# Attention, then a gated feed-forward block: another order of the kernel's 1094 steps, and one bias product in place of a mask product

## The chip, the cores and the metric

The kernel runs on one core of one Trainium2 chip. The metric is the time of one execution in microseconds of device time: the kernel before takes 238.46 us (median of 3 runs, 238.38 to 238.53).

## What is computed

The first half is attention over 4 batches, 8 heads, 768 positions and 64 channels. A query sees the 96 positions up to and with its own and the first 8 positions of the sequence ("global" keys); each score carries a bias, minus a slope of the head times the distance. The second half takes the attention output as 3072 tokens of 512 channels through two 512 x 1536 products, multiplies `silu` of the one with the other, and through a 1536 x 512 product.

```python
scores = scale * np.matmul(q, k.transpose(0, 1, 3, 2))
keep = is_global | is_local
bias = -slopes[:, None, None] * dist[None, :, :]
scores = np.where(keep, scores + bias[None], -1000000000.0)
a = np.exp(scores - max); a = a / (sum(a) + 1e-09)
x = np.matmul(a, v)                     # -> (3072, 512)
g = x @ w_gate
out = (g / (1 + np.exp(-g))) * (x @ w_val) @ w_out
```

## The kernel before, in words

**Tiling.** Keys are cut into chunks of 120, each with the 8 global keys beside it. For a batch and a pair of heads the scores of all chunks lie in three or four units: four in batch 0, where a unit holds up to 432 columns for each of two heads, three in the later batches. Scores lie with the keys on the partitions, so the exponentials go straight into the product with `v`. The feed-forward half works on 8 blocks of 384 tokens (two to a batch) and 12 blocks of 128 hidden channels.

**Order.** Nothing schedules this program but the constant `ORDER` (L39 to L123): a list of 1094 steps, run from the first to the last (L715 to L717). Each step issues its instructions on one engine (a few on two), each engine and each DMA queue runs its own in the order in which they were issued, and waits only for data and for buffers. Another list is another order on every engine. The list also decides which of the 8 banks of PSUM a product gets: `single` and `double` (L225 to L241) hand out banks that a step earlier in the list gave back, so a product waits for the instruction that last read its bank.

**The steps**, with their line and engine. Numbers after the letter are batch or token block, pair of heads, unit, and so on.

- Loads: `Ld`, `Li`, `Lf.S` on the SyncE queue and `Lf.A` on the ScalarE queue (distance table, identity, and the first half of `q` and `k` of the heads 0 to 3 in float32; L252 to L259); `Lh`, `Lv`, `Lw`, `L4`, `Lr`, `Lo` on GpSimd's queue (the rest of `q` and `k` of batch 0, `v`, the weights, later batches; L262 to L319).
- `pre` (L323 to L326, VectorE): sets a tile of ones and zeroes parts of the key tiles. `zc` (L517, L518): zeroes the corners of the buffers for the exponentials, `zc.1` of five buffers in ten instructions. `Z` (L282): zeroes parts of a `v` tile.
- `fill.n` (L343, TensorE): n products of the tile of ones, which nobody reads; they keep TensorE at work while it has no data.
- `cast` (L347): float32 to float16 of what `Lf` loaded. `sl.h` (L329, VectorE): the identity times the slope of head h. `M.h.part` (L335, ScalarE): the mask of head h, the exponential of minus slope times distance; part 0 has 216 columns, part 1 has 432.
- `T` (L364, TensorE): six transposes of `q` or `k`; `k`, `q` (L377 to L383, L393): copy them out of PSUM, on the engine named at the end (V is VectorE, A is ScalarE, P is GpSimd). `G`: copies the global rows of `v` into the other chunks.
- `B.hp.u` (L461, TensorE): the bias of a unit of batch 0, slope-identity times distance table, summed into the scores' bank ahead of them. `c` (L481): the scores. `x` (L526, ScalarE): the exponential. `m` (L553, VectorE): the product with the mask, for the units that had no `B`. So every unit of batch 0 has either four small matmuls of `B` or one to two VectorE instructions of `m`.
- `w` (L585, TensorE): sums and weighted `v`; `i`, `r` (L604, L605, L611): the reciprocal of the sums, spread over the rows; `n` (L597): copies the weighted sums out; `p` (L621): multiplies them into the token block `xT`.
- `g`, `v` (L638, TensorE): gate and value product of a token block and a block of hidden channels, four matmuls each (`ga`, `gb`: the halves of a `g`); `t` (L644, ScalarE): tanh; `s` (L648, VectorE): silu, which frees the bank of `g` and the buffer of `t` (there are three); `h` (L654, VectorE): times the value product, which frees the bank of `v` and the buffer of `s`.
- `o` (L679, L668, TensorE): the product with `w_out`; `e` (L697, L688, L692): copies it out and stores it. `D`, `K`, `U`, `kw`, `qw`: keys and queries of the later batches, by DMA transposes or by TensorE.

In what follows the *head* is all that comes before step `g.0.3`, and the *stream* is the rest, where TensorE goes through the same kinds of product to the end.

Of the kernel before, what the change touches and what calls it, by code (L numbers as in the profile page):

```python
# [55 lines left out]
s.0.5 Lr.1.0.6 v.0.7 Lv.1.3 g.0.11 s.0.6 h.0.3 Lr.1.1.4 h.0.5 t.0.4 s.0.4 h.0.7 Lr.1.0.5 m.0.3.2.V
v.0.4 h.0.4 g.0.9 Lr.1.1.7 g.0.10 t.0.9 w.0.0.1.1 w.0.0.1.2 t.0.10 Lr.1.0.4 h.0.6 s.0.9 t.0.11
w.0.1.1.0 w.0.1.1.1 s.0.10 w.0.1.1.2 p.0.0.1.0.V Lo.2 i.0.1.1 v.0.2 p.0.0.1.1.V r.0.1.1 p.0.1.1.0.V
v.0.9 p.0.1.1.1.V Lr.2.0.0 v.0.10 g.0.8 v.0.11 g.1.4 g.1.6 t.0.8 D.1.2.0 s.0.8 h.0.9 Lr.2.0.1 g.1.1
h.0.10 t.1.4 t.1.1 h.0.2 g.1.8 s.1.4 g.1.5 s.0.11 U.0.0 U.0.1 D.1.2.1 s.1.1 U.1.1 t.1.8 U.1.0  # L60
Lr.1.0.7 h.0.11 v.1.4 s.1.8 t.1.6 kw.0.A v.1.6 qw.1.A kw.1.V g.1.0 s.1.6 v.1.8 h.1.4 qw.0.A h.1.6
t.1.0 Lv.1.2 s.1.0 c.1.0.1 c.1.1.0 v.0.8 g.1.9 t.1.5 h.1.8 x.1.1.0 s.1.5 t.1.9 x.1.0.1 v.1.1 g.1.2
h.0.8 o.0.1.0 D.1.3.0 s.1.9 c.1.1.1 Lr.3.0.1 c.1.0.0 x.1.1.1 Lr.2.1.3 v.1.0 h.1.1 o.0.0.0 o.0.1.1
x.1.0.0 g.1.7 t.1.2 t.1.7 v.1.9 Lr.2.0.2 Lr.2.0.3 h.1.0 m.1.0.0.V g.1.3 g.1.11 Lr.2.1.2 v.1.3 s.1.2
o.0.0.1 m.1.1.1.V v.1.11 o.0.0.2 t.1.11 o.0.1.2 s.1.7 m.1.0.1.V D.1.3.1 Lr.2.1.0 v.1.2 s.1.11 t.1.3
h.1.11 o.0.0.3 s.1.3 h.1.9 o.0.1.3 m.1.1.0.V w.1.0.0.2 w.1.0.0.1 h.1.3 e.0.0 h.1.2 K.1.2 w.1.0.0.0
c.1.2.1 e.0.1 c.1.2.0 o.0.2.0 n.1.0.0 x.1.2.1 i.1.0.0 g.1.10 Lr.2.0.5 K.1.3 r.1.0.0 x.1.2.0 v.1.5
Lr.2.1.5 o.0.2.1 o.0.2.2 h.1.5 t.1.10 Lv.1.4 c.1.3.1 p.1.0.0.0.V x.1.3.1 Lv.1.5 D.2.0.0 s.1.10
m.1.2.0.V m.1.2.1.V m.1.3.1.V c.1.3.0 v.1.7 Lv.1.6 v.1.10 o.1.0.0 o.0.2.3 x.1.3.0 e.0.2 Lr.2.1.4
D.2.1.0 m.1.3.0.V o.1.0.1 c.1.0.2 w.1.1.0.0 w.1.1.0.1 w.1.1.0.2 h.1.7 Z.2.P p.1.0.0.1.V o.1.1.0  # L70
o.1.0.2 x.1.0.2 h.1.10 Lr.3.0.0 i.1.1.0 c.1.2.2 c.1.1.2 Lr.2.0.4 n.1.1.0 K.2.0 x.1.2.2 c.1.3.2
o.1.1.1 x.1.3.2 r.1.1.0 o.1.1.2 Lr.2.1.1 Lr.2.1.6 D.2.1.1 p.1.1.0.1.V Lr.2.0.7 p.1.1.0.0.V o.1.0.3
m.1.2.2.V g.2.6 Lr.2.0.6 t.2.6 g.2.10 g.2.2 v.2.2 o.1.1.3 t.2.10 e.1.0 t.2.2 s.2.6 v.2.6 s.2.10
m.1.0.2.V g.2.0 g.2.5 m.1.3.2.V s.2.2 x.1.1.2 g.2.9 h.2.2 t.2.0 Lr.3.0.4 v.2.0 m.1.1.2.V h.2.6
w.1.0.1.1 w.1.0.1.0 w.1.0.1.2 t.2.5 Lr.3.1.4 Lv.2.4 s.2.5 s.2.0 w.1.1.1.1 e.1.1 w.1.1.1.0 Lv.2.0
n.1.0.1 i.1.0.1 w.1.1.1.2 Lr.3.1.1 Lr.3.0.5 o.1.2.0 g.2.7 r.1.0.1 t.2.9 D.2.0.1 i.1.1.1 D.2.2.0
v.2.7 n.1.1.1 t.2.7 r.1.1.1 Lr.2.1.7 o.1.2.1 Lr.3.1.0 s.2.7 g.2.3 t.2.3 p.1.1.1.0.V v.2.5 Lr.3.0.7
D.2.3.0 Lv.2.1 v.2.4 v.2.9 o.1.2.2 h.2.7 h.2.5 p.1.0.1.0.V Lr.3.0.2 s.2.9 h.2.9 Lr.3.0.3 o.1.2.3
# [28 lines left out]
h.5.0 o.4.2.0 m.3.0.2.V s.5.5 t.5.3 t.5.2 s.5.3 o.4.0.3 g.6.0 v.5.11 s.5.2 h.5.11 v.5.3 m.3.2.2.V
t.5.9 v.5.1 s.5.6 o.4.2.1 h.5.1 g.5.4 h.5.3 o.4.2.2 s.5.9 v.5.2 v.5.9 m.3.3.2.V h.5.2 o.4.2.3 h.5.9
g.6.8 g.6.11 t.5.4 v.5.5 e.4.0 g.6.10 t.6.0 s.6.0 t.6.8 s.5.4 h.5.5 w.3.1.1.0 w.3.0.1.1 w.3.0.1.0
w.3.0.1.2 s.6.8 e.4.2 w.3.1.1.1 i.3.1.1 w.3.1.1.2 v.6.8 i.3.0.1 t.6.10 n.3.0.1 v.5.4 g.6.2 n.3.1.1  # L110
# [642 lines left out]
```

## Time and profile before

| | |
|---|---|
| time, median of 3 runs | 238.46 us (238.38 to 238.53) |
| the profiled execution | 238.79 us |
| its span, first to last instruction | 237.0 us |
| TensorE (PE) busy | 229.5 us, 97% |
| VectorE (DVE) busy | 173.8 us, 73% |
| ScalarE (ACT) busy | 138.0 us, 58% |
| GpSimd (POOL) busy | 77.6 us, 33% |
| moved by DMA | 25.54 MB |

The span is 1.8 us shorter than the execution's own time. The profile shows each matmul from its start to a modelled end, so that matmuls overlap: a busy PE says that none of them was waited for longer than the tail of the one before, and only the distance from one start to the next tells how fast they go. PEld, the loading of weights, overlaps PE. In rows of the timeline, the first two numbers are the start and the length in us, "x6" are six instructions in one row, and a bracket at the end gives idle time ahead of the row and what ended it.

### The profile page before, as it was taken

The page shows a single profiled execution, that of the slowest core. Times are in us where ns is not written, and L with a number is a line of the kernel's source. Part 1 is how long each engine was busy: PE and PEld are TensorE (multiplying, and loading weights), DVE is VectorE, ACT ScalarE, POOL GpSimd, SP SyncE. Part 2 cuts the span into 40 slices and gives each one's busy share as a digit, 9 for nine tenths or more (in the row PEclk, how much of TensorE's full clock was granted, in tenths as well). Part 3 has the DMA queues.
Part 4 walks back from the last instruction along what each step waited for, and adds up shares of the span by engine and source line. Part 5 has one row for each costly group of instructions (what it writes and reads, how often), then busy time and mean ns, then how long its engine had stood idle before and what let it go on. Part 6 is the DMA issues. An engine that isn't in the chain of part 4 may idle for free.

```text
span 237.0 us, 6183 instructions
## 1 busy us (share of the span) xinstructions
PE 229.5 (97%) x2520; PEld 132.3 (56%) x2520; DVE 173.8 (73%) x428; ACT 138.0 (58%) x251; POOL 77.6 (33%) x102
## 2 busy tenths in 40 slices
PE   3999999999999999999999999999999999999994
PEld 2655666655555655555655564565556655555442
DVE  6799898948786888877988988776679984364400
ACT  6699632792889624778983389969334222412131
POOL 8975585540969774665300000000000000000000
PEclk9999999999999999999999999999999999999999
DMA  7999999999999999999995150011011000110034
GB/s 177 181 182 207 193 198 186 176 176 162 139 130 153 178 165 139 141 167 112 139 192 55 44 80 27 20 47 47 0 44 48 3 1 0 44 47 0 8 125 177
DMA packets 88196, 25.54 MB, mean 108 GB/s; under 512 B 78016, under 2 KB 85224, under 8 KB 88168
## 3 DMA queue, kind: packets, MB, share of 16 engines
q0 software_dynamic: 66992, 13.77, 74.6%
q1 hardware_dynamic: 20488, 10.80, 24.9%
q10 hardware_dynamic: 688, 0.59, 0.7%
q8 instruction: 19, 0.31, 0.5%
q14 instruction: 9, 0.07, 0.1%
HBM read 28.51 MB, written 6.29 MB: 147 GB/s over the span
## 4 chain that ended last, share of the span: by engine, by line
PE 94%; DVE 3%; ACT 1%; issue 1%; DVEq 0%
PE banks L638 53%; PE banks L679 26%; PE banks L585 6%; PE banks L481 4%; PE banks L343 2%; PE banks L668 1%; PE banks L364 1%; ACT at L526 1%; PE banks L461 1%; PE banks L402 1%; DVE at L518 0%; DVE rb L611 0%; DVE at L517 0%; DVE dT L604 0%; DVE xT L621 0%
## 5 line engine op out<-in xcount | busy, mean ns | idle before, releaser
L644 ACT ACTIVATE th<-banks 128x384 f32<-128x384 f32 x96 | 44.1, 491 | 60.1 <-PE banks L638 54.6
L638 PE MATMUL banks<-xT,wv 128*128 128x384 f16 x384 | 73.3, 326 | 0.0
L638 PE MATMUL banks<-xT,wg 128*128 128x384 f16 x384 | 72.1, 326 | 0.0
L654 DVE TENSOR_TENSOR hT<-banks,sl 128x384 f16<-128x384 f32 x96 | 51.3, 551 | 24.0 <-PE banks L638 22.2
L679 PE MATMUL banks<-wo,hT 128*128 128x512 f16 x276 | 68.5, 379 | 0.0
L526 ACT ACTIVATE at<-banks 64x640 f16<-64x640 f32 (+4 forms) x88 | 62.3, 714 | 5.3 <-PE banks L481 4.3
L648 DVE SCALAR_TENSOR_TENSOR sl<-th,banks 128x384 f32<-128x384 f32 x96 | 50.8, 547 | 12.6 <-ACT th L644 11.6
L638 PEld LDWEIGHTS <-wg 128*128 128x128 f16 x384 | 37.3, 98 | 27.0
L638 PEld LDWEIGHTS <-wv 128*128 128x128 f16 x384 | 36.4, 98 | 26.6
L679 PEld LDWEIGHTS <-hT 128*128 128x128 f16 x276 | 26.1, 98 | 26.5
L553 DVE TENSOR_TENSOR at<-at,masks 128x864 f16<-128x864 f16 (+5 forms) x62 | 26.1, 459 | 4.5 <-ACT at L526 4.4
L267 POOL DMA_DIRECT2D vS<-in_v_dram x28 | 25.0, 899 | 10.3 <-DMA vS<-in_v_dram 3.0
L697 ACT ACTIVATE osb<-banks 128x512 f32<-128x512 f32 x23 | 13.6, 597 | 22.1 <-PE banks L679 18.4
L305 POOL DMA_DIRECT2D kst<-in_k_dram x20 | 16.7, 841 | 14.1 <-DMA kN<-kst 8.8
L305 POOL DMA_DIRECT2D qst<-in_q_dram x20 | 16.8, 846 | 7.5 <-DMA qst<-in_q_dram 2.6
L481 PE MATMUL banks<-qT,kT 64*64 64x160 f16 (+9 forms) x408 | 13.3, 227 | 0.2 <-DVE xT L621 0.2
L481 PEld LDWEIGHTS <-kT 64*64 64x64 f16 (+1 forms) x408 | 7.9, 104 | 8.9 <-issue 7.6
L621 DVE TENSOR_TENSOR xT<-ns,rb 128x384 f16<-128x384 f32 x24 | 12.5, 550 | 0.3
L585 PE MATMUL banks<-at,vS 128*32 128x216 f16 (+6 forms) x576 | 12.0, 225 | 0.1
L597 ACT COPY ns<-banks 128x768 f32<-128x768 f32 x12 | 9.4, 801 | 4.5 <-PE banks L585 4.2
L604 DVE STREAM_TRANSPOSE dT<-banks 128x384 f32<-128x384 f32 x16 | 9.2, 574 | 3.1 <-PE banks L585 2.8
L585 PEld LDWEIGHTS <-vS 128*32 128x32 f16 x576 | 10.0, 95 | 2.3 <-issue 1.5
(59 smaller groups left out, 116.7 us busy)
## 6 DMA issues: line engine op xcount, KB each, us to landing
out_dram<-osb SPq DMA_DIRECT2D x23, 256.0 KB, 2.1
vS<-in_v_dram POOLq DMA_DIRECT2D x24, 120.0 KB, 8.0
qst<-in_q_dram POOLq DMA_DIRECT2D x20, 96.0 KB, 8.5
kst<-in_k_dram POOLq DMA_DIRECT2D x20, 96.0 KB, 7.9
wg<-in_moe_w_gate_dram POOLq DMA_DIRECT2D x6, 256.0 KB, 9.3
wv<-in_moe_w_val_dram POOLq DMA_DIRECT2D x6, 256.0 KB, 8.3
wo<-in_moe_w_out_dram POOLq DMA_DIRECT2D x3, 512.0 KB, 10.3
k<-in_k_dram POOLq DMA_DIRECT2D x3, 192.0 KB, 6.3
```

The lines of the kernel that those rows point to most:

```text
L267: nc.gpsimd.dma_start(out=v_of(b)[r0:r0 + n, c, :, :], in_=v[b, :, KC * c:KC * c + n, :].rearrange("h p d -> p h d"))
L305: nc.gpsimd.dma_start(out=rows_of(i, b, h // 2)[:, :, h % 2, :], in_=KQ[i][b, h].rearrange("(t p) d -> p t d", p=128))
L481: nc.tensor.matmul(sc[k0:k1, hi, col + a:col + z], lhsT=keys[r, k0:k1], rhs=qTs[b, hp][r, q0 + a:q0 + z], start=fresh, stop=True, skip_gro ...
L526: nc.scalar.activation(out=of(at), in_=of(sc), func=AF.Exp, scale=scale)
L553: ENG[e].tensor_mul(a2, a2, m[:, :, m0:m0 + n])
L585: nc.tensor.matmul(dst[r, o:o + n], lhsT=vSs[b][:, c, 4 * g + j, what - 1::2] if what else ones[:, 0:32], rhs=ats[b, hp, u][:, j % 2, col: ...
L638: nc.tensor.matmul(gv[t, f, which][:, 0:TB], lhsT=w[:, c, 128 * f:128 * f + 128], rhs=xTs[t][:, c, :], start=(c == 0), stop=(c == NC - 1))
L644: nc.scalar.activation(out=th, in_=gv[t, f, 0][:, 0:TB], func=AF.Tanh, scale=0.5)
L648: nc.vector.scalar_tensor_tensor(out=sl, in0=gv[t, f, "t"], scalar=1.0, in1=gv[t, f, 0][:, 0:TB], op0=AluOp.add, op1=AluOp.mult)
L654: nc.vector.tensor_mul(hTs[t][:, f, :], gv[t, f, 1][:, 0:TB], gv[t, f, "s"])
L679: nc.tensor.matmul(ops_t[t, i], lhsT=hTs[t][:, f, 128 * i:128 * i + 128], rhs=wo[:, f, :], start=(f == 0), stop=(f == NFF - 1))
L697: nc.scalar.mul(out=osb, in_=ops, mul=0.5)
```

## The change

Only `ORDER` is changed. The list has 1094 steps before and after. In batch 0, `B.0.1` and `B.2.1` come in, and `B.3.1` goes; `m.0.0.1.V` and `m.0.2.1.V` go, and `m.0.3.1.V` comes in: one bias product more, one mask product less. All other steps are the same, in another sequence from the first line to the last. The part that is spoken of most is the beginning (before, then after):

```diff
-Ld.S Z.0.P Z.3.P Lf.A.1.1 Li zc.0.V Lh.0.0.4.8 zc.1.V Lf.A.1.0 Lh.1.0.4.8 pre cast.1.1.V Lf.S.0.1
-M.5.1 M.0.0 sl.3 Lf.S.0.0 M.2.1 Lh.1.1.0.4 fill.14 sl.7 M.1.0 sl.6 Lh.0.1.0.4 Z.1.V sl.2 cast.0.1.V
-M.7.0 T.1.0.1 B.1.1 q.1.0.V M.3.1 cast.1.0.P T.1.0.0 Lh.1.1.4.8 cast.0.0.A M.2.0 fill.2 Lv.0.1
-k.1.0.V sl.1 M.7.1 T.0.0.0 T.2.0.0 k.0.0.V Lv.0.0 T.3.0.0 sl.0 k.3.0.V M.4.1 M.5.0 B.1.0 M.0.1
-T.0.0.1 c.0.1.1 Lh.0.1.4.8 sl.4 T.2.0.1 M.3.0 c.0.1.0 q.0.0.V x.0.1.1 Lv.0.2 q.2.0.V T.1.1.1 T.3.0.1
-M.6.0 B.0.0 k.2.0.V x.0.1.0 Lv.0.3 c.0.0.0 sl.5 M.1.1 Lw.0.0.1 c.0.0.1 T.1.1.0 x.0.0.1 q.3.0.V M.4.0
...
-w.0.0.1.0 s.0.2 t.0.0 s.0.0 c.0.3.3 Lw.1.2.0 x.0.2.3 i.0.0.1 c.0.3.2 v.0.0 g.0.3 t.0.1 x.0.3.3
...
+Lf.A.1.1 Ld.S Lf.A.1.0 Z.0.P M.6.1 pre Li M.0.1 Z.3.P Lh.1.0.4.8 Lf.S.0.1 zc.1.V Lf.S.0.0 Z.1.V
+zc.0.V Lh.0.0.4.8 fill.14 cast.1.1.V Lh.0.1.0.4 sl.3 T.1.0.1 sl.2 M.3.1 M.2.1 sl.5 Lh.1.1.0.4
+cast.1.0.P cast.0.1.V q.1.0.V sl.6 B.1.0 B.1.1 M.7.1 sl.1 sl.0 cast.0.0.A Lv.0.0 M.1.1 T.1.0.0
+T.0.0.1 M.5.1 fill.2 T.0.0.0 T.3.0.1 k.1.0.V sl.7 k.0.0.V Lv.0.3 c.0.1.1 T.2.0.1 M.5.0 c.0.1.0 M.2.0
+x.0.1.1 q.3.0.V M.7.0 x.0.1.0 q.2.0.V B.0.1 q.0.0.V Lh.1.1.4.8 M.0.0 T.3.0.0 T.2.0.0 T.0.1.0 sl.4
+c.0.0.1 k.2.0.V Lh.0.1.4.8 T.1.1.0 B.0.0 Lv.0.2 c.0.0.0 x.0.0.1 B.2.0 M.3.0 c.0.2.0 M.1.0 T.0.1.1
+k.3.0.V x.0.0.0 Lv.0.1 Lw.0.0.0 k.1.1.V Lw.0.0.1 B.2.1 x.0.2.0 c.0.2.1 T.1.1.1 x.0.2.1 M.4.0 k.0.1.V
+zc.2.V w.0.0.0.0 c.0.3.1 M.6.0 B.3.0 q.0.1.A c.0.3.0 T.2.1.1 x.0.3.1 G.0.1.4.V x.0.3.0 B.0.2 c.0.0.2
+q.1.1.V T.2.1.0 Lw.1.0.0 i.0.0.0 T.3.1.0 M.4.1 q.2.1.A Lw.1.0.1 Lw.0.1.1 m.0.3.1.V r.0.0.0 Lw.0.1.0
+x.0.0.2 w.0.1.0.0 c.0.1.3 i.0.1.0 Lw.1.1.0 w.0.0.0.1 w.0.0.0.2 w.0.1.0.1 r.0.1.0 x.0.1.3 p.0.0.0.0.V
+Lw.1.1.1 w.0.1.0.2 p.0.0.0.1.V c.0.0.3 k.3.1.A p.0.1.0.1.V k.2.1.A T.3.1.1 q.3.1.A G.0.4.7.S c.0.2.2
+ga.0.2 x.0.2.2 p.0.1.0.0.V ga.0.1 x.0.0.3 ga.0.0 c.0.1.2 m.0.1.3.V x.0.1.2 m.0.2.2.V m.0.0.3.V
+gb.0.2 gb.0.0 t.0.0 c.0.3.3 c.0.2.3 Lw.0.2.0 t.0.2 m.0.1.2.V s.0.0 x.0.2.3 Lv.0.6 Lw.0.2.1 gb.0.1
+v.0.0 s.0.2 w.0.0.1.0 c.0.3.2 h.0.0 v.0.3 x.0.3.3 g.0.3 Lv.0.5 t.0.1 x.0.3.2 g.0.6 m.0.2.3.V g.0.7
...
+s.5.9 o.4.2.0 g.5.4 t.5.5 m.3.3.2.V t.5.11 v.5.11 h.5.3 v.5.1 s.5.11 t.6.8 h.5.11 o.4.2.1 h.5.1
+o.4.2.2 s.5.5 t.5.4 v.5.5 w.3.1.1.2 s.5.4 s.6.8 t.6.2 w.3.1.1.1 n.3.1.1 w.3.1.1.0 w.3.0.1.2 h.5.5
...
```

On the engines: VectorE begins with `pre` and not with `zc.0` and `zc.1`, and takes its first `cast` after `zc.1`, `Z.1` and `zc.0`. The loads on the ScalarE queue and on the SyncE queue keep their sequence in the head. GpSimd's queue has `q` ahead of `k` at the first two `Lh`, `k` ahead of `q` at the next two, and `Lv.0.0` and `Lv.0.3` first of the four early parts of `v`. ScalarE has five masks of part 1 ahead of `cast.0.0.A` where it had three of each part, and four masks instead of six between that cast and its first `x`. From `g.0.3` on, TensorE has 364 steps before and after, the same ones but for a `v.0.3` in the head where `v.0.1` was.

More of the change, by code (lines that the diff above doesn't have):

```diff
@@ L56 @@
[L56 to L66, printed above, removed]
@@ L107 @@
[L107 to L110, printed above, removed]
-r.3.0.1 r.3.1.1 t.6.11 v.5.6 v.6.11 s.6.10 v.6.0 t.6.2 p.3.1.1.0.V h.5.4 h.6.8 g.6.7 v.6.10 s.6.2
-g.6.4 g.6.1 t.6.7 p.3.0.1.0.V s.6.11 g.6.5 p.3.1.1.1.V h.5.6 s.6.7 v.6.4 p.3.0.1.1.V t.6.5 h.6.10
@@ new lines @@
+t.4.7 o.3.0.0 o.3.2.3 x.3.1.0 m.3.0.1.V o.3.0.1 g.5.10 v.4.7 s.4.7 t.5.10 h.4.7 e.3.2 o.3.0.2
+c.3.0.0 c.3.3.0 o.4.1.0 s.5.10 m.3.2.1.V o.4.1.1 x.3.0.0 m.3.1.1.V x.3.3.0 m.3.2.0.V m.3.1.0.V
+m.3.3.0.V g.4.9 c.3.3.1 o.3.0.3 t.4.9 v.5.10 Lv.3.6 Lv.3.5 g.4.11 e.3.0 m.3.0.0.V g.5.8 s.4.9 g.5.7
+x.3.3.1 t.4.11 v.4.9 h.5.10 v.4.11 o.4.1.2 s.4.11 m.3.3.1.V w.3.0.0.1 h.4.9 t.5.7 s.5.7 h.4.11
+w.3.1.0.2 w.3.0.0.2 w.3.0.0.0 i.3.0.0 n.3.0.0 w.3.1.0.0 w.3.1.0.1 i.3.1.0 n.3.1.0 o.4.1.3 o.4.0.0
+e.4.1 c.3.1.2 c.3.0.2 o.4.0.1 t.5.8 x.3.0.2 o.4.0.2 s.5.8 g.5.0 v.5.0 o.4.0.3 r.3.1.0 c.3.3.2
@@ new lines @@
+g.7.6 s.7.10 g.7.8 v.7.3 t.7.3 v.7.9 t.7.8 h.6.1 s.7.4 g.7.1 v.7.8 g.7.7 s.7.8 h.7.9 o.6.0.0 s.7.3
+g.7.5 t.7.7 s.7.7 v.7.10 g.7.11 h.7.8 t.7.6 t.7.5 o.6.0.1 o.6.2.0 h.7.10 t.7.11 s.7.6 h.7.3 v.7.1
+v.7.4 o.6.1.0 o.6.2.1 t.7.1 s.7.1 h.7.1 g.7.2 v.7.2 o.6.2.2 h.7.4 s.7.5 t.7.2 s.7.2 s.7.11 v.7.6
+o.6.1.1 h.7.2 o.6.1.2 v.7.7 o.6.0.2 h.7.6 o.6.0.3 o.7.1.0 e.6.0 v.7.5 h.7.5 o.7.0.0 o.6.1.3 e.6.1
+h.7.7 v.7.11 o.6.2.3 o.7.0.1 h.7.11 o.7.1.1 o.7.0.2 o.7.0.3 e.6.2 o.7.1.2 o.7.1.3 o.7.2.0 e.7.0
+o.7.2.1 o.7.2.2 o.7.2.3 e.7.1 e.7.3 e.7.2
```

114 lines of the change are left out of this document (55 added, 59 removed).

## Prediction

> **What bounds the kernel now.** I read the busy line of the page first, then the busy time of two stretches (bounds and length; busy us and count of PE, PEld, DVE, ACT, POOL; then clock and DMA).
>
> ```profile
> PE 229.5 (97%) x2520; PEld 132.3 (56%) x2520; DVE 173.8 (73%) x428; ACT 138.0 (58%) x251; POOL 77.6 (33%) x102
> ...
> 9.60:20.40 10.80, 10.12 (x233) 6.39 (x230) 10.36 (x38) 9.70 (x25) 8.39 (x12) 1.00 1.67 187
> 25.39:233.40 208.01, 208.01 (x2175) 118.78 (x2174) 152.10 (x344) 117.09 (x207) 57.05 (x69) 1.00 0.98 97
> ```
>
> Two regimes. From `g.0.3` at 25.39 to the last products PE is busy 208.01 of 208.01 us and waits for nobody: the stream is PE's own work, and no order of DVE, ACT or DMA can shorten it. In the head nobody is slack: between 9.60 and 20.40 PE, DVE and ACT are each busy for 9.7 to 10.4 of 10.80 us. So an order can gain in the head, lose in the stream by a new wait, and change the stream by one thing more:
>
> ```profile
> 45.60 0.81 PE L638 MATMUL banks<-xT,wv 128*128 128x384 f16 x4
> 46.34 0.47 PE L481 MATMUL banks<-qT,kT 64*64 64x160 f16 x16
> 46.75 0.82 PE L638 MATMUL banks<-xT,wv 128*128 128x384 f16 x4
> 47.41 0.81 PE L638 MATMUL banks<-xT,wg 128*128 128x384 f16 x4
> ```
>
> Four products take 0.65 from start to start (47.41 less 46.75 is 0.66), but 0.74 when the next matmul uses another tiling of the array (128*128 to 64*64). A switch of tiling costs PE 0.09.
>
> **The change part by part.** *The stream.* From `g.0.3` both lists hold 364 PE steps of the same kinds and sizes. I counted neighbours of another tiling: 53 before, 52 after. That is -0.09.
>
> *The front of DVE.* Rows of before:
>
> ```profile
> 0.82 0.15 DVE L517 MEMSET at<- 64x112 uint32 x1 [0.82 <-PEq L734]
> 1.25 0.15 DVE L517 MEMSET at<- 64x112 uint32 x1
> 3.45 0.27 DVE L323 MEMSET ones<- 128x256 f16 x1
> 4.04 0.62 DVE L347 CAST q<-q 128x384 f16<-128x384 f32 x1
> 4.59 0.73 DVE L329 TENSOR_SCALAR slopeI<-ident 128x128 f16<-128x128 f16 x3
> 5.41 0.64 DVE L282 MEMSET vS<- 32x256 uint32 x2
> 5.97 0.48 DVE L329 TENSOR_SCALAR slopeI<-ident 128x128 f16<-128x128 f16 x1
> 6.01 0.63 DVE L347 CAST k<-k 128x384 f16<-128x384 f32 x1
> ...
> 3.78 3.17 PE L343 MATMUL banks<-ones 128*128 128x256 f16 x14 [3.78 <-DVE ones L323]
> 6.88 0.53 PE L364 MATMUL banks<-ident,q 128*64 128x128 f16 x6
> ```
>
> `pre` goes from 3.45 to 0.82, so the ones are there at 1.09 and the fills, which start 0.06 behind them, run from 1.14 to 4.26 (14 take 3.1). That alone gains nothing, since nobody reads them; but before, the first transposes stood behind the fills until 6.88, with `q` cast since 4.66. After, they wait for the cast alone: 0.82, plus `pre` 0.59 (3.45 to 4.04), `zc.1` 2.20 (1.25 to 3.45), `Z.1` 0.56 (5.41 to 5.97), `zc.0` 0.43 (0.82 to 1.25) is 4.60; the cast's 0.62 and a hop of 0.05 make 5.28. `T.1.0.1` comes **1.60 earlier**. The cast of `k` waits for its load as before and ends near 6.5, ahead of its transposes.
>
> *PE to the first scores.*
>
> ```profile
> 7.34 0.47 PE L461 MATMUL banks<-dist,slopeI 128*128 128x144 f16 x4
> 7.74 0.53 PE L364 MATMUL banks<-ident,k 128*64 128x128 f16 x6
> 8.20 0.61 PE L343 MATMUL banks<-ones 128*128 128x256 f16 x2
> 8.74 1.08 PE L364 MATMUL banks<-ident,k 128*64 128x128 f16 x18
> 9.75 0.54 PE L461 MATMUL banks<-dist,slopeI 128*128 128x432 f16 x2
> 10.22 0.36 PE L364 MATMUL banks<-ident,q 128*64 128x128 f16 x6
> 10.51 0.25 PE L481 MATMUL banks<-qT,kT 64*128 64x144 f16 x4
> ...
> 10.80 0.45 ACT L526 ACTIVATE at<-banks 128x336 f16<-128x336 f32 x1 [1.10 <-PE banks L481]
> ```
>
> These rows hold a clock that doubles: the 14 fills take 0.22 each for 256 columns and the 18 transposes 0.056 each (to 9.75), while the six at 10.22 take 0.29 less one switch, 0.033 each, and the 432 columns at 9.75 take 0.19. I put the step at 9.6 and, for the forecast, leave it there. After, at half clock: `T` 0.46, `B.1.0` moved ahead, 0.72 (two times 432 columns at the rate of the fills), `B.1.1` 0.40, two `T` 0.78, `fill.2` 0.54, two `T` 0.78: 3.68. `c.0.1.1` starts at 5.28 + 3.68 = 8.96 (before 10.51), and its exponential, 0.3 to 0.4 later, near 9.3 instead of 10.80: **1.5 earlier**.
>
> *ACT gives most of it back.*
>
> ```profile
> 11.15 0.38 ACT L335 ACTIVATE masks<-dist 128x216 f16<-128x216 f16 x1
> 11.43 0.88 ACT L526 ACTIVATE at<-banks 128x864 f16<-128x864 f32 x1
> 12.20 0.56 ACT L335 ACTIVATE masks<-dist 128x432 f16<-128x432 f16 x1
> ...
> 22.38 0.87 ACT L644 ACTIVATE th<-banks 128x384 f32<-128x384 f32 x2
> ...
> 10.80:22.37 11.57, 10.89 (x236) 6.91 (x235) 11.12 (x37) 11.50 (x26) 8.20 (x13) 1.00 1.60 191
> ```
>
> From its first exponential to the first tanh at 22.38 ACT is busy 11.50 of 11.57 us. A narrow mask costs 0.28 there (11.15 to 11.43), 0.10 less than its length, so a wide one 0.46. Before, two of each stand in this stretch, 1.48; after, six narrow and one wide, 2.14: +0.66. And ACT now runs ahead of PE: it is free for `x.0.1.0` at 9.9, but `c.0.1.0` stands behind six transposes at half clock and ends at 10.1; laying the queues out step by step I find 0.27 there and 0.5 more in four smaller waits, where before has 0.3 in all. So 1.5 - 0.66 - 0.5 leaves about **0.35** at the first tanh.
>
> *DVE.* `m.0.0.1` and `m.0.2.1` go (0.28 each to the next start, of 0.36 to 0.39), `m.0.3.1` comes: -0.28 of DVE time between 14 and 17, bounds 0 and -0.4. It buys nothing by itself, since ACT and PE are no later than DVE there. The bias product that pays for it is four matmuls, 0.30 with its switch, in a stretch where PE is waiting for banks anyway; if that cover were gone it would cost 0.30.
>
> *PE at the end of the head.*
>
> ```profile
> 20.39 0.35 PE L481 MATMUL banks<-qT,kT 64*128 64x168 f16 x5 [0.18 <-DVE xT L621]
> ...
> 25.39 0.81 PE L638 MATMUL banks<-xT,wg 128*128 128x384 f16 x4
> ```
>
> Before, PE's last wait ends at 20.39, for a bank that the second `p` frees, and 5.00 of work lie between it and `g.0.3`. After, the last wait is for the bank of `ga.0.1`, which the copy `q.3.1` frees at about 20.15; by then one half product (0.33) and the scores of `c.0.0.3` (0.13) are done, so 4.53 are left: `g.0.3` at 24.7, 0.7 earlier. The same laying out for before gives 25.2 where the trace has 25.39, so I take **-0.5** for the head, with bounds of -0.7 and -0.2 (three of the slope tiles took 0.1 to 0.4 longer at 4.59 and 5.97 than the rest, and may again).
>
> *A wait that the stream gets.* Steps `h.5.1 s.5.5 t.5.4 s.5.4 s.6.8` and `w.3.1.1.0` hang together: `t` has three buffers, so `t.5.4` waits for `s.5.5`, which DVE takes behind `h.5.1`, and the bank of `w.3.1.1.0` is the one `s.6.8` frees.
>
> ```profile
> L654 DVE TENSOR_TENSOR hT<-banks,sl 128x384 f16<-128x384 f32 x96 | 51.3, 551 | 24.0 <-PE banks L638 22.2
> L648 DVE SCALAR_TENSOR_TENSOR sl<-th,banks 128x384 f32<-128x384 f32 x96 | 50.8, 547 | 12.6 <-ACT th L644 11.6
> L644 ACT ACTIVATE th<-banks 128x384 f32<-128x384 f32 x96 | 44.1, 491 | 60.1 <-PE banks L638 54.6
> ...
> 178.58 0.49 PE L585 MATMUL banks<-at,ones 128*32 128x72 f16 x20
> 178.90 0.48 PE L585 MATMUL banks<-at,vS 128*32 128x72 f16 x20
> ```
>
> Behind the last matmul of `v.5.1`: its tail and a hop 0.2, `h` 0.47 and the second last `s` 0.47 to the next start (0.08 less than their length), the other two `s` and `t` their length and a hop of 0.03 to 0.05, 0.58, 0.60 and 0.52: 2.84. PE has, until it wants the bank, two `o` and a `v`, 0.65 each (an `o` is as many columns as a `v`), and two `w` of 0.32 (178.58 to 178.90) with a switch: 2.68. A wait of some 0.2, and more if DVE is late at `h.5.1`; bounds 0 and 0.5, I take **+0.25**. Every other bank and buffer of the stream I checked in the same way has cover at least like the shortest of before, or short of it by 0.25 at most.
>
> *Loads.*
>
> ```profile
> L312 POOL DMA_DIRECT2D wv<-in_moe_w_val_dram x2: 716/716/716, 12.3 to 13.2; - x2
> ...
> DMA to landing us min/median/max: 8.2/8.3/8.5
> ...
> 23.15 0.81 PE L638 MATMUL banks<-xT,wv 128*128 128x384 f16 x4
> ```
>
> These two are the first block of the value weights, landed by 21.7; they are GpSimd's 13th and 14th load before and after. PE wanted them at 23.15 and will want them at 22.7: 1.0 of cover. The sequence of the other early loads changes by one or two places of about 1 us, and none is wanted sooner than that; 0, unless the queue slips by 1.
>
> *Sum:* -0.5 - 0.09 + 0.25 = -0.34. The profiled execution takes 238.79, of which 237.0 are the span, and would take 238.45; against the median of the runs, 238.46, it gives **238.1**.
>
> **The rivals.** *The clock is granted earlier.* It came 5.8 after the first fill (3.78 to 9.6); if that is what counts, it comes near 7.0. PE then does 2.6 us of the list, about 1.75 of them without switches, in 0.87 less, but ACT is busy with masks until 8.9, so the first exponential gains 0.4 and two waits of 0.1 to 0.2 go: -0.55, **237.55**. Against it: PE now stands idle from 4.26 to 5.28, which it never did before. *The waits are fewer:* without the one in the stream, and with 0.6 in the head, **237.8**.
>
> *The clock is granted later: the slower side.* The hole of 1.02 us starts the count afresh, and what follows it is transposes instead of fills. With the grant at 13.0, PE does 3.4 us at half clock, some 2.2 of them without switches: 2.2 later, of which its waits behind (0.59, 0.18, 0.16, 0.05 by my laying out) swallow 1.0; +1.2, **239.3**. That is 0.37 per us, so the gain is gone from a grant at 10.5 on. For it: the hole; against it: the rows at 8.74 to 9.75 are mostly transposes, and the clock was granted in them.
>
> [...]
>
> *The stream takes more waits than one.* Several covers are a little shorter than before's shortest; two or three waits of 0.3 and a late load give +0.9, **239.0**. *The mask that goes is what pays:* then the gain would be DVE's 0.28 and the rest of the order neutral, 238.2, not to be told from the forecast by the time alone.
>
> **How the numbers follow.** A measurement of this kernel can tell about 0.2%, 0.48 us, from no change: the borders are 237.98 and 238.94. Forecast 238.1 (238.0 to 238.6, with the mask rival) 0.40; clock earlier 0.22; fewer waits 0.15; clock later 0.13; waits in the stream 0.10. So faster 0.37, within 0.2% 0.40, slower 0.23. The range, 237.4 to 239.0, takes in the first three and half of the waits; by itself the forecast's is 237.9 to 238.6.
>
> **What would show it.** In the profile of after: the first row of L364 at 5.3; the first L526 near 9.3; the 432 columns of L461 at 0.36 each ahead of the clock's step and 0.19 behind it, and where the step lies; the first tanh near 22.0; the 12 products of `g.0.3` on starting near 24.7 to 24.9; PE waiting once in the stream, near 175, and the stretch from `g.0.3` to the last product within 0.3 of 208. I am wrong if the step of the clock moves by over 1 us, if `g.0.3` is not before 25.2, or if PE waits in the stream for more than 0.5 in all.

## The result, and the profile of the kernel after

The kernel after takes **239.71 us** (median of 19 executions, 238.73 to 241.81), the kernel before 238.46 beside it (237.86 to 239.90): a ratio of **1.0054, 95% interval 1.0034 to 1.0075**. It is slower by half a per cent, where 238.1 was forecast. Run again on two chips, the unchanged kernel after stood at 1.0017 (0.9993 to 1.0041) and 1.0043 (1.0014 to 1.0072). An execution over 1.5% slower than the fastest of its kernel is left out of a ratio: one of `e_narrow28` and one of `e_wide10` below.

The profiled execution took 239.73 us, of which 237.0 are the span, the same span as before. The page of after: its span; busy time, share and number of instructions by engine; and the queue `instruction`, taken for the one that brings code (transfers, MB, share).

```profile
span 237.0 us, 6196 instructions
PE 230.9 (97%) x2524; PEld 132.6 (56%) x2524; DVE 174.0 (73%) x426; ACT 139.3 (59%) x251; POOL 77.2 (33%) x102
...
q8 instruction: 19, 0.31, 0.6%
```

The 2524 products and as many weight loads are four more of each than before (2520): the net bias product. The timeline of the head:

```profile
1.19 3.17 PE L343 MATMUL banks<-ones 128*128 128x256 f16 x14 [1.19 <-DVE ones L323]
4.72 0.65 DVE L347 CAST q<-q 128x384 f16<-128x384 f32 x1
5.43 0.53 PE L364 MATMUL banks<-ident,q 128*64 128x128 f16 x6 [1.08 <-DVE q L347]
9.41 0.36 PE L364 MATMUL banks<-ident,q 128*64 128x128 f16 x6
9.52 0.45 ACT L526 ACTIVATE at<-banks 128x336 f16<-128x336 f32 x1 [0.24 <-PE banks L481]
...
22.16 0.87 ACT L644 ACTIVATE th<-banks 128x384 f32<-128x384 f32 x2
24.93 0.33 PE L638 MATMUL banks<-xT,wg 128*128 128x384 f16 x1
```

The head did what was forecast for it: first transpose at 5.43 (5.28), a hole of 1.08 ahead of it (1.02), first exponential at 9.52 (9.3), first tanh at 22.16 (22.0), `g.0.3` at 24.93 (24.7 to 24.9) where before had 25.39. The six transposes take 0.53 at 5.43 and 0.36 at 9.41; in this execution the trace has the full clock from 9.41 on (before: from 9.60).

The gain of 0.46 is gone by 88 us. The stream again, cut where TensorE stands still (the columns are those of the table of stretches above), and the timeline there:

```profile
24.93:87.12 62.19, 62.19 (x775) 36.69 (x773) 51.84 (x120) 39.27 (x69) 41.87 (x52) 1.00 1.73 171
87.65:233.40 145.75, 145.75 (x1399) 82.02 (x1400) 100.03 (x224) 78.98 (x138) 14.93 (x18) 1.00 0.53 68
```

```profile
86.63 0.65 PE L638 MATMUL banks<-xT,wg 128*128 128x384 f16 x3
...
87.65 0.60 PEld L638 LDWEIGHTS <-wg 128*128 128x128 f16 x5 [0.75 <-issue]
87.65 0.82 PE L638 MATMUL banks<-xT,wg 128*128 128x384 f16 x4 [0.37 <-issue]
```

TensorE is 100% busy on both sides, and between them it stops in the middle of step `g.2.11`, behind three of its four products: 0.69 us from start to start where 0.16 is usual. What ends the idle time is "issue": the profile shows nothing that TensorE waited for, no data, no bank, no semaphore. The last product ends at 233.96, before at 233.94. So in this execution the head's gain and one hole cancel, and what makes it longer than before's is time outside the span (2.73 us, before 1.79), which unchanged kernels have too: 5 of 29 executions of before that ran beside the first experiments had 2.0 to 3.7. But the median of the 19 spans is 237.6, and 236.7 for those 29 of before. The profiled execution doesn't show this difference; the experiments had to.

### The profile page after: what moved, and what is told of

Its sections match the earlier page's. It is cut to its first block, busy times and chain, and to the rows that moved or that the text cites. A ratio compares the mean times of both kernels' runs of the same rounds, so it can differ in the third digit from the quotient of the medians.

```text
span 237.0 us, 6196 instructions
## 1 busy us (share of the span) xinstructions
PE 230.9 (97%) x2524; PEld 132.6 (56%) x2524; DVE 174.0 (73%) x426; ACT 139.3 (59%) x251; POOL 77.2 (33%) x102
## 4 chain that ended last, share of the span: by engine, by line
PE 93%; DVE 3%; ACT 2%; issue 1%
PE banks L638 54%; PE banks L679 26%; PE banks L585 6%; PE banks L481 4%; ACT at L526 2%; PE banks L668 1%; PE banks L364 1%; PE banks L461 1%; PE banks L402 1%; ACT masks L335 0%; DVE qT L393 0%; DVE at L518 0%; DVE at L517 0%; ACT qT L393 0%; DVE q L347 0%
## 5 line engine op out<-in xcount | busy, mean ns | idle before, releaser
L644 ACT ACTIVATE th<-banks 128x384 f32<-128x384 f32 x96 | 45.1, 491 | 61.9 <-PE banks L638 57.8
L553 DVE TENSOR_TENSOR at<-at,masks 128x864 f16<-128x864 f16 (+5 forms) x60 | 25.6, 465 | 2.6 <-ACT at L526 2.4
L481 PE MATMUL banks<-qT,kT 64*64 64x160 f16 (+8 forms) x408 | 13.9, 228 | 0.1
```

Source lines behind the costliest of these rows:

```text
L481: nc.tensor.matmul(sc[k0:k1, hi, col + a:col + z], lhsT=keys[r, k0:k1], rhs=qTs[b, hp][r, q0 + a:q0 + z], start=fresh, stop=True, skip_gro ...
L553: ENG[e].tensor_mul(a2, a2, m[:, :, m0:m0 + n])
L644: nc.scalar.activation(out=th, in_=gv[t, f, 0][:, 0:TB], func=AF.Tanh, scale=0.5)
```

## The experiments

Each was timed in five rounds beside the kernel before on the same chip; the ratios are to that. "The span's rest" is the time from the end of the last product to the end of the span.

### Both kernels again; the hole in the head filled; the constants late

No edit for the first two. The third and the fourth edit the list of after:

```diff
e_fill19:   -fill.14
            +fill.19
e_late_pre: -... Z.0.P M.6.1 pre Li ... zc.0.V Lh.0.0.4.8 fill.14 ...
            +... Z.0.P M.6.1 Li ... zc.0.V Lh.0.0.4.8 pre fill.14 ...
```

> The kernel before, unchanged, for the spans and granted clocks of many executions, of which only one is known so far (span 237.0 in an execution of 238.79). Theory 1, the clock: the new head loses the granted clock in some executions, this one does not. Then its mean clock is 1.0 in every execution, and the spans lie within 0.7 of each other, near 236.7. Theory 2, the stream: the new order costs PE time behind the head in every execution. Then the spans of this kernel are about 0.6 below those of the changed one at clock 1.0 (median 237.3), whatever the clock does. Theory 3, the time outside the span: nothing of the order shows; then this kernel too has executions with 2.4 to 2.9 outside its span, as often as the changed one (5 of 19).

> The changed kernel again, for a second profile and more executions. Theory 1: about 4 in 10 executions have a mean clock under 1.0 and spans of 237.8 to 239.1, the others 1.0 and 236.7 to 237.6. Theory 2: the idle 0.5 of PE at 87, put down to issue, is there again at the same product. If it is not there, it belongs to that one execution. Ratio to the kernel before 1.003 to 1.007 in any case.

> The changed kernel with 19 fills instead of 14, so that PE has no hole between the fills and its first transposes. Theory 1, the hole costs the clock: mean clock 1.0 in every execution, the executions of 238 to 239 in the span are gone, median about 0.7 below the changed kernel, near 238.4 to 239.0. Theory 2, the stream: 0.0 to 0.2 off the changed kernel. If the early fills and not the hole are at fault, executions with a clock under 1.0 remain.

> The changed kernel with the step that sets the ones back behind the zeroing of the corners, right ahead of the fills, as it stands before: the fills start near 4.8 and end near 7.9, and the first transposes stand behind them. The gain of 0.46 at the end of the head goes, and more (the fills end 1.0 later than before's). Theory 1: mean clock 1.0 in every execution; spans near 238, in a narrow band; median within 0.3 of the changed kernel's, since it gains the lost clock back and loses the head. Theory 2: slower than the changed kernel by 1 to 1.5.

Measured: before against itself 1.0005 (0.9984 to 1.0026); after 1.0017 (0.9993 to 1.0041); 19 products 0.9981 (0.9963 to 1.0000); late constants 1.0076 (1.0048 to 1.0104). The unchanged before repeats to 0.05%, with an interval of 0.2% to either side. The kernel after, at 1.0017, came out below the 1.003 to 1.007 that was expected in any case, and its interval on this chip takes in 1; in the first run and in `c_after2` below it doesn't. Three things follow. The half per cent of the first run is no fixed amount. The early constants are worth 1.85 us to this order (240.79 against 238.94; the theory of the clock had expected at most 0.3): without them `g.0.3` starts at 26.70, later than before, so all that the new head gains hangs on them. And the hole at "issue" came back in both other traces of this list, before the same instruction; with 19 products it was 0.22 long and stood one step earlier, in `o.1.2.0`, and counted in instructions of TensorE at the same place: 2241 lie ahead of it in all of them.

The four traces also differ in the end of the span. The chain of waits at the end (start, us, what), of c_after and then of before:

```profile
230.20 0.60 ACT osb L697
230.80 0.02 issue
230.82 4.36 DMA out_dram<-osb
...
235.28 0.49 ACT osb L688
```

```profile
230.67 0.97 PE banks L668 x6
231.65 0.65 PE banks L679 x3
232.29 1.66 PE banks L668 x18
233.95 0.02 issue
233.97 0.29 DVE osb L692
```

In before the last products set the end. In c_after an output transfer takes 4.36 us from issue to landing, and the last copy (L688), which needs its buffer, starts at 235.28, 1.3 us behind the last product. What runs beside it shows the view of the DMA queues from 230.8 to 235.2 (GB/s in 40 slices, then the queues):

```profile
GB/s 0 0 0 0 0 0 0 130 261 503 428 335 354 317 56 0 0 0 0 168 317 410 335 372 410 205 37 0 19 0 19 19 19 37 19 19 37 19 19 37
...
q1 hardware_dynamic: 286, 0.52, 32.1%
q8 instruction: 1, 0.02, 2.7%
```

One transfer of code, 16 KB, falls into this stretch, and from there on the output trickles at 19 to 37 GB/s. The whole trace of c_after has 20 such transfers on this queue, that of before 19.

### The clock's windows, and the bias part undone

No edit for c_after2. The others, on the lists of before, before and after:

```diff
e_before_pre26: -Ld.S Z.0.P ... pre ... fill.14     (before)
                +pre Ld.S Z.0.P ... fill.26
e_before_pre20: the same with fill.20
e_fill19_masks: -B.0.1 -B.2.1 -m.0.3.1.V, fill.14   (after)
                +m.0.0.1.V +m.0.2.1.V +B.3.1, fill.19
```

> The kernel after, unchanged, for more executions of it and a second look at the stream. Theory W (windows): the granted clock steps up at the end of the first window of 3.41 us in which TensorE has no hole; the windows' phase differs from execution to execution. In the four traces at hand the step lies at the end of the first such window. With the hole of 1.0 us after the 14 warm-up products (4.35 to 5.43), W expects a step at 8.8 to 11.3 us, or, for about one phase in six, a step near 4.5 that is lost again for one or two windows: then the mean granted clock is 0.993 or 0.986 and the span about 1 us longer. Theory S (stream): the hole of 0.5 us near 87 us comes back in every trace of this kernel, before the same TensorE instruction (number 2243 counted from the start). The rival, chance: the hole near 87 was of two traces only, and the mean clock stays above 0.995 in all executions.

> The kernel before with the nine constants (pre) first on VectorE and 26 warm-up products in place of 14, so that they run from 1.2 to 6.95 us without a hole and all that follows stays where it is in the kernel before. Theory W: every window from 1.2 us on is full, the clock steps up at 4.6 to 8.0 us in place of 7.2 to 10.6, 2.6 us earlier in the mean; at the 0.2 to 0.35 us of span per us of step that the traces show, 0.5 to 0.9 us shorter than the kernel before: ratio 0.996 to 0.998. Rival H (the head is bound by its data, not by the clock): under 0.2 us gained, ratio 0.999 to 1.000.

> The kernel before with pre first and 20 warm-up products: they end near 5.6 us, and the first transpose may start 1.3 us earlier than before (its cast ends near 4.7 to 5.3). Theory W: as with 26 as long as no hole of over 0.3 us opens behind the products; if the keys of the next transpose are late, a hole opens and part of the gain is lost again. W with no hole: 0.6 to 1.1 us shorter than before, ratio 0.9955 to 0.9975. Rival H: the head's data set its pace, and an earlier first transpose alone gives nothing: ratio 0.999 to 1.000.

> The kernel after with 19 warm-up products and the part on biases undone: mask products for units (0,1) and (2,1) of batch 0 and a bias product for (3,1), as in the kernel before, so one bias product less on TensorE and one mask product more on VectorE. The part costs little by all theories: TensorE saves about 0.2 us of products in the head, VectorE does one product of about 0.5 us more. Expected within 0.2 us of the 19 products with the new biases (238.21 us in the earlier runs, 0.998 of the kernel before). Rival B (the bias part is what costs): 0.4 us or more shorter than that, ratio under 0.9965.

Measured: after 1.0043 (1.0014 to 1.0072); 26 products 1.0012 (1.0002 to 1.0022); 20 products 1.0059 (1.0045 to 1.0073); masks 1.0050 (1.0033 to 1.0066). Of the second and third no theory had expected that they are slower than before. The fourth was expected within 0.2 us of the 19 products with the new biases (238.21), or, by its rival B, 0.4 or more below them; it came out 1.4 above, which neither had. The clock came near the places that W had named for it, 8.8 to 11.3 or near 4.5. The first transposes of c_after and of c_after2, one kernel, one list:

```profile
5.43 0.53 PE L364 MATMUL banks<-ident,q 128*64 128x128 f16 x6 [1.08 <-DVE q L347]
```

```profile
5.43 0.36 PE L364 MATMUL banks<-ident,q 128*64 128x128 f16 x6 [1.08 <-DVE q L347]
```

The full clock was there at 10.26 in the first, at 5.01 in the second. The 3.41 us of W is a length that the clock's records show: the full clock lasts 228.69 us in before and in after, 67 times 3.41, and once 3.41 in `e_wide10` below. W had expected a step near 4.5 to be lost again for a window or two; this one, at 5.01, was not. c_after2 has `g.0.3` at 23.83 and its last product's end at 232.87, 1.1 earlier than before, and the span is 237.0 all the same. The same in the others: with 20 products the last product ends at 233.22, 0.7 earlier than before, and the span is 238.3. So the clock's gain was there, and the end of the span ate it. The table shows the ten traces taken so far, in the order of TensorE's instructions (products, weight loads and 14 others):

| trace | instructions | 20th transfer of code | slowest of the last output transfers | span's rest |
|---|---|---|---|---|
| before, c_before | 5054 | none | 2.16 | 3.08, 3.09 |
| e_late_pre | 5062 | none | 2.04 | 3.06 |
| after | 5062 | 238.75, behind the end | 2.03 | 3.06 |
| c_after | 5062 | 231.79 | 4.36 | 4.71 |
| c_after2 | 5062 | 230.61 | 3.74 | 4.09 |
| e_fill19_masks | 5064 | 230.89 | 3.83 | 4.19 |
| e_before_pre20 | 5066 | 230.59 | 4.19 | 5.06 |
| e_fill19 | 5072 | 229.40 | 2.86 | 3.55 |
| e_before_pre26 | 5078 | 229.99 | 2.84 | 3.74 |

That gave **theory C**: what counts is how many instructions TensorE has. A few more, and one more block of code is fetched, beside the last output.

### The same work in fewer or more instructions

```diff
e_wide7, e_wide10 (after), e_before_wide (before, pre first):
-    nc.tensor.matmul(warm[:, 0:256], lhsT=ones[:, 0:128], rhs=ones[:, 0:256],
+    nc.tensor.matmul(warm[:, 0:512].rearrange("p (a c) -> p a c", a=2),
+                     lhsT=ones[:, 0:128], rhs=ones.unsqueeze(1).broadcast_to([128, 2, 256]),
e_wide7: fill.14 -> fill.7;  e_wide10: -> fill.10;  e_before_wide: -> fill.13;  all: fill.2 -> fill.1
e_narrow28 (before): 128 columns in place of 256, fill.14 -> fill.28, fill.2 -> fill.4
```

> The kernel after, with its 14 + 2 warm-up products of 256 columns issued as 7 + 1 of 512 columns: the same warm-up time, the same hole from 4.4 to 5.4 us, 8 products and 8 weight loads fewer (TensorE's count of instructions goes from 5062 to 5046; the kernel before has 5054). Theory C (code): TensorE's code arrives in transfers of 16 KB; with 5062 instructions and more a 20th transfer is fetched at about 230 us, and the output transfers that run beside it land 0.8 to 2.3 us later (six traces with it: 2.8 to 4.4 us from issue to landing; four without: 2.0 to 2.2). C expects no 20th transfer before the end, output transfers of 2.0 to 2.2 us, about 3.1 to 3.3 us from the last product's end to the end of the span in every execution, and 0.3 to 0.8 us less than the kernel after in the median. Rival W alone (the clock's windows make the difference): nothing changes, median span as in the kernel after, 237.2 to 237.6.

> The kernel before, with its 14 + 2 warm-up products of 256 columns issued as 28 + 4 of 128 columns: the same warm-up time within 0.1 us, 16 products and 16 weight loads more (5054 to 5086 instructions on TensorE). Theory C: the 20th transfer of code comes at about 230 us, an output transfer beside it lands 0.8 to 2.3 us late, and the span grows by 0.5 to 1.7 us: ratio 1.002 to 1.007. Rival (only the head and the stream matter): no change, ratio 0.999 to 1.001.

> The kernel after with 10 + 1 warm-up products of 512 columns in place of 14 + 2 of 256: the hole behind the products is filled as with 19 products of 256 columns, and TensorE has 5052 instructions. Theories W and C together: first transpose at 5.4 to 5.7 us without a hole ahead of it, no lost windows, no 20th transfer of code, the last product near 232.5 to 233.2, 3.1 to 3.3 us from there to the end, span 235.7 to 236.4: ratio to the kernel before 0.995 to 0.998. C wrong: as with the 19 products of 256 columns, 0.998.

> The kernel before with pre first and 13 + 1 warm-up products of 512 columns, so TensorE has 5050 instructions: the run with 26 products of 256 columns again, without the 24 instructions that it added. That run ended 0.25 us later than the kernel before although its last product ended 0.7 us earlier. Theory C: no 20th transfer of code, output transfers of 2.0 to 2.2 us, span 0.5 to 0.8 us shorter than before: ratio 0.9965 to 0.998. C wrong: ratio 1.000 to 1.002 as with the 26.

Measured: e_wide7 **0.9982** (0.9960 to 1.0004), e_narrow28 **1.0035** (1.0015 to 1.0055), e_wide10 0.9969 (0.9949 to 0.9989), e_before_wide 0.9976 (0.9963 to 0.9988). All four went the way that C expected, two kernels with fewer warm-up instructions on after's list, one on before's, and one with more. e_wide7 is the kernel after in every other step, with eight warm-up products where it has 16 and the same hole (first transpose at 5.45). Its page, its stream and the chain at its end (its lines stand two further down, so that L670 is L668):

```profile
PE 229.1 (97%) x2516; PEld 130.7 (55%) x2516; DVE 174.2 (74%) x426; ACT 139.2 (59%) x251; POOL 77.1 (33%) x102
...
q8 instruction: 19, 0.31, 0.6%
```

```profile
24.30:232.46 208.16, 208.16 (x2179) 119.03 (x2177) 152.50 (x344) 118.59 (x207) 57.24 (x71) 1.00 0.89 100
```

```profile
230.17 2.63 PE banks L670 x24
232.81 0.02 issue
232.83 0.29 DVE osb L694
```

No 20th transfer, no hole in the stream (208.16 of 208.16), a span's rest of 3.06. Of its 12 spans ten lie between 235.4 and 236.5, and the other two, 237.6 and 238.3, have mean clocks of 0.993 and 0.986; the spans of the kernel after, in its 40 executions, lie between 236.3 and 239.2. e_narrow28 is before with 16 products and 16 weight loads more, the same columns in all; its page has the 20th transfer

```profile
PE 228.7 (97%) x2536; PEld 132.7 (56%) x2536; DVE 173.6 (73%) x428; ACT 137.9 (58%) x251; POOL 77.3 (33%) x102
...
q8 instruction: 20, 0.33, 0.6%
```

and the 11 spans in its ratio spread from 236.4 to 238.9 (before: 236.1 to 237.4). In the profiled execution the collision was slight (a rest of 3.19), so how much it costs differs from one execution to the next. e_before_wide, the kernel of e_before_pre26 with 28 instructions fewer, went from 1.0012 to 0.9976.

The profiled execution of e_wide10 happens to show a clock that is lost. It took 241.34 us, where the median of the twelve is 237.97. TensorE waited 0.9 and 0.6 us for casts of `k` there. The stretches of its head (the last three columns are clock, DMA, GB/s):

```profile
1.20:6.60 5.40, 5.40 (x18) 1.89 (x19) 3.89 (x25) 3.65 (x6) 5.29 (x9) 1.00 1.02 216
6.60:10.10 3.50, 2.07 (x40) 1.33 (x38) 2.29 (x10) 1.37 (x4) 3.39 (x5) 0.99 1.63 179
10.10:13.50 3.40, 3.17 (x43) 2.10 (x40) 3.05 (x12) 2.82 (x9) 2.74 (x5) 0.50 1.93 174
13.50:16.90 3.40, 3.40 (x26) 1.20 (x24) 2.64 (x12) 2.21 (x4) 2.48 (x4) 0.50 1.78 183
16.90:20.30 3.40, 3.40 (x80) 2.04 (x78) 2.17 (x6) 3.20 (x9) 2.11 (x3) 1.00 1.25 206
```

Granted at 6.64, kept for 3.41 us (TensorE is busy 2.07 of 3.50 in that stretch), then at 0.50 for the next two stretches. The last product ends at 236.51, 3.4 later than with e_before_wide.

### What was still open: the bias part alone, and the last hole

Both are e_wide10 with another list:

```diff
e_wide10_masks: -B.0.1 -B.2.1 -m.0.3.1.V
                +m.0.0.1.V +m.0.2.1.V +B.3.1
e_wide10_B:     -c.0.1.0 ... B.0.1 ... T.3.0.0 T.2.0.0 T.0.1.0
                +c.0.1.0 ... T.3.0.0 T.2.0.0 B.0.1 T.0.1.0
```

> The kernel after with 10 + 1 warm-up products of 512 columns (237.97 us and 0.9969 of the kernel before in the earlier runs) and the part on biases undone: mask products for units (0,1) and (2,1), a bias product for (3,1). With 19 products of 256 columns the same edit cost 1.4 us, but both of those kernels had the 20th transfer of code near 230 us, so the end of the span could not be told from the head there; this one has 5044 instructions on TensorE and should have none. In the traces with 19 products the first product of the stream started at 24.73 without the new biases and at 23.96 with them, with the clock stepping up at 5.3 and 6.45. Theory B (the part on biases is worth about 0.8 us in the head, because two mask products on VectorE stood ahead of the first value products): 0.6 to 1.0 us longer than with the new biases, ratio to the kernel before 0.9995 to 1.0015. Rival (it was the end of the span that differed): within 0.3 us, ratio 0.9960 to 0.9982.

> The kernel after with 10 + 1 warm-up products of 512 columns and the bias product of unit (0,1) moved behind the two key transposes that follow it, so that they run while it waits for its bank (0.2 to 0.4 us of TensorE hole ahead of that product in four traces). Theory W: fewer holes in the window of 7 to 10.5 us, so the clock is lost less often: no execution with a mean clock of 0.986, and up to 0.2 us less in the median, ratio 0.995 to 0.997. Rival: the transposes only move the wait to their own banks and the exponential of unit (0,1) comes later: 0 to 0.2 us more, ratio 0.997 to 0.999.

Measured: masks 0.9990 (0.9979 to 1.0002), B 0.9972 (0.9961 to 0.9984), on one chip 238.21 and 237.73 us. So the bias part is worth 0.4 to 0.5 us in the head: not the 1.4 that the kernels with the 20th transfer showed, less than the 0.6 to 1.0 of theory B here, and more than the 0.3 of its rival. The first mask product and the first sums, without the new biases and then with them (`e_wide10_B`, which has `B.0.1` moved besides; lines stand two further down here too):

```profile
13.43 0.40 DVE L555 TENSOR_TENSOR at<-at,masks 128x288 f16<-128x288 f16 x2
13.45 0.54 PEld L587 LDWEIGHTS <-ones 128*32 128x32 f16 x16
...
16.53 0.37 PE L587 MATMUL banks<-at,ones 128*32 128x216 f16 x8
...
22.26 0.87 ACT L646 ACTIVATE th<-banks 128x384 f32<-128x384 f32 x2
```

```profile
13.22 0.44 PE L587 MATMUL banks<-at,ones 128*32 128x216 f16 x16
...
15.98 0.44 PE L587 MATMUL banks<-at,ones 128*32 128x216 f16 x16
...
21.35 0.87 ACT L646 ACTIVATE th<-banks 128x384 f32<-128x384 f32 x2
```

The masks' trace is 0.23 late at the first sums, 0.55 at the next and 0.91 at the first tanh; 0.35 was there ahead of the edit (first exponential 9.27 and 8.92), so about 0.5 to 0.6 come behind it. Moving `B.0.1` left the median where e_wide10 had it; none of its nine executions lost the clock, against one of twelve, too few to say that the move did it. e_wide10, e_wide10_B and e_before_wide beat both kernels of this case.

## Why the prediction was wrong, point by point

- **What failed** is a sentence of the first part, "the stream is PE's own work, and no order of DVE, ACT or DMA can shorten it", with what the sum made of it: that only banks, buffers and loads can make TensorE wait, and that all behind the last product stays as it was. The description of the kernel has the same gap, where an engine "waits only for data and for buffers". The sum had no term for TensorE's own code, and four products more are eight instructions more (5062 for 5054). In its place the runs showed a hole of 0.5 us near 87 us, in all four traces of this list (0.50 to 0.55, and 0.75 with the late constants), and 1.0 and 1.65 us at the end in two of three traces of the kernel after. With 16 instructions fewer (`e_wide7`), the same order has neither, and measured 0.9982; the forecast of 238.1 against 238.46 was 0.9985.
- **The hole at 87.** In all 16 traces of this study the instruction with 2241 others ahead of it starts 1.40 us or more after the eighth transfer of code landed (read from the records of the transfers); in the five with a hole it starts 1.40 to 1.62 after it. Before has 2.42 and 2.52 there, and e_wide7, where the same step order meets that place 16 instructions later, 2.61. That the hole is code not yet there is read from this, and no run changed the transfer alone. A thin margin doesn't always come with a hole: e_fill19_masks has 1.50 and e_wide10 1.41, both without one. So the hole goes with the place of the steps as well as with their number, and why the margin is thin in the new order stays open. In the five traces with a hole the eighth transfer starts when TensorE has started 2212 to 2224 instructions, in the others at 2194 to 2214. The 120 small products of `w` at 80.1 to 81.9 us don't set the orders apart: before has as many, at 80.6 to 82.3.
- **The end.** Shown by seven traces with the 20th transfer ahead of the end (rest 3.19 to 5.06) and nine without (3.06 to 3.09), and by e_wide7 and e_narrow28, which cut the same warm-up columns into fewer or more instructions. Why one transfer of 16 KB holds the output up for so long no view shows. Why the order's own list, at 5062, fetches it in some executions and not in others is open; it lies between 5054, where no trace has it, and 5064, where all have it.
- **Head, -0.5:** right, -0.46 in the profiled execution, and by the named steps: the copy `q.3.1` ends at 20.29 (20.15), `ga.0.1` starts at 20.34, and 4.59 of work follow (4.53). But its clock term, "for the forecast, leave it there" (9.6), was a coin's toss: unchanged kernels had the step at 8.10 and 9.60 (before), at 5.01, 9.41 and 10.26 (after). The full clock lasts 228.69 or 232.11 us in 15 of the 16 traces, 3.42 apart and 67 or 68 times 3.41, and in e_wide10 once 3.41 and then 221.87, 65 times. In windows of that length, counted back from the step itself, the step lies in all 16 traces at the end of the first one in which TensorE was busy for 0.79 or more; the window ahead of it was busy for 0.71 or less. So a window with holes was enough, where W had asked for none.
- **The rival "clock granted later"** named the right place, the hole of 1.02, and the wrong mechanism. The hole doesn't start a count afresh: c_after2 was granted the clock at 5.01, inside it. It makes the windows that it falls into less busy (after: 0.68 from 2.58 to 5.99), and a clock already granted was taken back in one trace: behind a window busy for 0.58 it was lost (e_wide10, with other holes), behind windows of 0.69 to 0.73 it was not (e_wide7, e_wide10_masks, e_before_pre20). Of the 40 executions of after, 8 have a mean clock of 0.986 to 0.991, and of the 116 of before none (0.998 or more); by an estimate from the 3.41 us and a span of 237, one window at half makes 0.993 and two make 0.986. With the hole filled (e_fill19) none of 12 is below 0.997; e_wide7, which has the hole, has two. That it is this hole in those executions is still argued, since no trace is of one of them. In the first 19, six of the 8 have spans of 237.8 to 239.1, and the others a median of 237.3; so of the 0.9 between the median spans of after and before about 0.3 goes with the lost clock. How often it is lost is no constant of the kernel: six times in the first 19 executions, twice in the next 21. No run shows the grant at 13.0 from which the 239.3 was added up: in the three traces of the kernel after it came at 5.01, 9.41 and 10.26. The price of 0.37 us per us of grant was too high (its own 1.2 over 3.4 is 0.35): after's last product ends 1.1 earlier for a grant 4.4 earlier, 0.25.
- **Transposes instead of fills.** The rival held it against the new head that transposes follow the hole. At the end of the window from 6.85 to 10.26 of c_after the clock was granted, and without its transposes that window would be 0.47 busy; at the end of the window from 2.77 to 6.18 of before, busy for 0.71 with warm-up products alone, it was not. So by these two traces the transposes count for the clock.
- **The wait at `w.3.1.1.0`, +0.25:** didn't come; TensorE's waits in the stream of e_wide7 are nil. **Switches, -0.09:** 208.27 from `g.0.3` to the last product's start in e_wide7, 208.33 in before: -0.06, right in sign and about in size.
- **The mask that goes, "It buys nothing by itself":** wrong; with the bias product that pays for it, it is worth 0.4 to 0.5 us.

## What to carry to other kernels

In this kernel TensorE runs 5054 instructions before and 5062 after, is busy for 97% of the span, and the page's queue `instruction` has 19 or 20 transfers of 16 KB: 19 with 5046 instructions (e_wide7), 20 with 5086 (e_narrow28). In such a kernel, count an engine's instructions before and after a change, look at the number of code transfers on the page, and see what runs beside the last one. Warm-up work, which nobody reads, did better here in few and wide instructions: with 16 fewer after's order measured 0.9982 (1.0017 to 1.0054 in three runs as it was), with 32 more before's 1.0035 (1.0005). And one profiled execution is not the kernel: list the spans and mean clocks of all of them before a trace is taken for the time.

## What the runs showed of the hardware

- A transfer of 16 KB of code took 0.9 to 1.9 us (0.89 to 1.69 in the traces of before and after, 1.9 near the end of c_after), and in six of seven traces output transfers that ran beside one at the end took 2.8 to 4.4 us instead of 2.0 to 2.2 (in the seventh 2.3).
- The list of after had the full clock from 5.01, 9.41 or 10.26 us on in three executions, so that the same six transposes at 5.43 take 0.53 us in c_after and 0.36 in c_after2.
- In e_wide10 a clock once lost came back after 6.83 us (10.06 to 16.89), though TensorE was busy 3.17 of 3.40 us from 10.10 on; a share of 0.79 had been enough for the first grant elsewhere. That is not explained.
